# Other order for the weight preparation and the first FFN units in a fused attention and gated FFN kernel

## The chip, the cores and the metric

The kernel runs on one core of one Trainium2 chip. The metric is the device time of one execution in microseconds (us), here the median of three runs. A profiled execution gives the trace from which durations are read. The engines are TensorE (PE in the profile, PEld for its weight loads), VectorE (DVE), ScalarE (ACT), GpSimd (POOL) and SyncE (SP); SP and ACT also issue the transfers.

## The reference, cut to what matters

Eight sequences with eight heads each (64 heads of 576 positions by 64) go through causal attention with a cumulative bias, and all 4608 tokens then through a gated FFN of width 1536:

```python
scores = scale * np.matmul(q, k.transpose(0, 1, 3, 2))
cum = np.cumsum(np.maximum(s, 0.0), axis=-1)
bias = -(cum[:, :, :, None] - cum[:, :, None, :])
scores = np.where(causal, -1000000000.0, scores + np.minimum(bias, 0.0))
attn = np.exp(scores - np.max(scores, axis=-1, keepdims=True))
attn = attn / (np.sum(attn, axis=-1, keepdims=True) + 1e-09)
x = np.matmul(attn, v).transpose(0, 2, 1, 3).reshape(B * S, H * D)
gate = 1.0 / (1.0 + np.exp(-(x @ w_gate)))
return ((gate * (x @ w_val)) @ w_out).astype(np.float32)
```

The three FFN weights arrive as 64-bit floats; the kernel reads them as integers and builds 32-bit floats from their upper halves on the chip.

## The kernel before, in words

**Attention.** One loop over ticks drives everything, five ticks to a head, one for each row tile of the scores, 320 in all. Heads 0 to 7 go through a 32-bit path with transposes on PE. Heads 8 to 63 use operands split into two 16-bit parts: L460 and L461 are the two score matmuls of a piece (six pieces to a head, named s12_3_0 for head 12, tile 3, first column 0), L485 takes the row maximum on DVE, L488 the exponential on ACT, L492 and L497 make the two parts of p, L508 turns p into pt by a transposing DMA on SP, and L520 to L525 multiply pt by v into one PSUM bank, av_bank. L415 swaps halves of the transposed q and k (T). There are two pt buffers of each kind, one buffer of p and one of e. So the maximum of head 12 cannot write e before p of head 11 is made, that not before the transposes of head 10 have read p, and those not before AV of head 8 has freed pt.

**FFN.** The tokens are cut into 18 groups of 256, and a unit is one group and one of twelve slices of 128 of the width. A unit has 24 matmuls 128x256 (L671, into PSUM gv, two buffers), a tanh on ACT (L676), t2 on DVE (L678), the split of the hidden value (L686 ACT, L687 DVE) and, in its "out", six matmuls 128x512 (L701). The first 24 units (groups 0 and 1, named gv0_0 to gv1_11) are written from tick NE = 44 on, FPT slices a tick, in both groups; their t2 wait in one large buffer (t2f) until every weight scale is known (`hidden_scale`), and then the 24 outs follow in a row. All later units follow a fixed share of tokens.

**Weights.** There are 18 weight steps: twelve for w_gate and w_val of a slice, six for two slices of w_out. A step loads 1 MB into a raw buffer (L253 and L260; on SP for the first two steps, on ACT's queue after that), decodes it (L271 on ACT, L273 on DVE), bounds its size (eight Gram matmuls into av_bank, L281 on PE, a row maximum L284 on DVE, a matmul with ones L286 on PE, small DVE steps L129 and L131) and splits it into 16-bit parts (L306 on ACT, L307 on DVE). Before, `weight_step` does all this for step n in one call. The raw buffers are ws0, three pieces of the room that w_out's parts take later (w2all), and two pieces of t2f; the twelve gate steps come first, then the six of w_out. In heads 0 to 7 `min(2 + n // 8, 6)` steps are written by tick n; the others come with the first units, WLA = 3 ahead.

**What orders the work.** The instructions are written in program order by the loop and then placed by a scheduler that runs a model of the time; `first(...)` gives a piece of code a high priority in it, `keep_in_program_order` holds an instruction at its place. `with first(NE <= n < NOFF)` gives it to s_part, av_part and x_part for ticks 44 to 86. Each engine, and SP's and ACT's issue of transfers, is in order.

**x.** The attention output of two heads goes through x16 (a transposing DMA) into one of NX = 10 x slots. NXE = 5 exist from the start, the other five after the first 24 outs (`late_slots`).

Of the kernel before, what the change touches and what calls it, by code (L numbers as in the profile page):

```python
# [25 lines left out]
def tile_attention_then_gated_ffn(  # L26
# [49 lines left out]
    w2all = w2room[:, : 48 * P].bitcast(F16).rearrange("p (f l h x n) -> p f l h x n", f=NF // 2, l=2, h=8, x=2)  # L76
# [113 lines left out]
    ones = lp.tile([P, P], F32, name="ones")  # L190
    nc.gpsimd.memset(ones, 1.0)
    NX, NXE = 10, 5
# [17 lines left out]
    t2big = cp.tile([P, 2 * NF * GT + 4], F32, name="t2f")  # L210
# [10 lines left out]
    raw = [lp.tile([P, RW], I32, name="ws0")] + [w2room[:, i * RW : (i + 1) * RW] for i in range(3)]  # L221
    raw += [t2big[:, 8 * GT + i * RW : 8 * GT + (i + 1) * RW].bitcast(I32) for i in range(2)]
    tops = [lp.tile([P, 8 * P], I32, name="wa0"), rows_out.bitcast(I32)]
# [6 lines left out]
    def room(n):  # L230

        o, f = wsteps[n]
        return outroom[f // 2] if o else (f % 4, n - 3)

    def load_weight(n):
        o, f = wsteps[n]
        fs = slice(f * P, (f + 1) * P)
        r = raw[room(n)[0]]
        for x, src in enumerate((w_out,) if o else (w_gate, w_val)):
            src = src[f * P : (f + 2) * P, :] if o else src[:, fs]  # L240
# [5 lines left out]
            if o == 0:  # L246
                src = src.rearrange("(c p) n -> p c n", p=P)
                dst = dst.rearrange("p (c x n) -> p c x n", c=NC, x=2)[:, :, x]
            else:

                src = src.rearrange("(x p) (h n) -> x p h n", p=P, h=8)
                dst = dst.rearrange("p (h x n) -> x p h n", x=2, h=8)
                ins = nc.scalar.dma_start(dst[0], src[0])  # L253
                if n < NF + 2:
                    tc.keep_in_program_order(ins)
                src, dst = src[1], dst[1]
            if n < 2:
                nc.sync.dma_start(dst, src)
            else:
                ins = nc.scalar.dma_start(dst, src)  # L260
                if n == 2 or NF <= n < NF + 2:
                    tc.keep_in_program_order(ins)

    def decode_weight(n):

        r = raw[room(n)[0]]
        if not wide:
            return r[:, : 8 * P].bitcast(F32), None
        a = tops[n % 2]
        top = a.bitcast(F16).rearrange("p (n t) -> p n t", t=2)[:, :, 1]  # L270
        nc.scalar.activation(top, r.bitcast(BF16)[:, 4:].rearrange("p (n t) -> p n t", t=4)[:, :, 0], AF.Copy)  # L271
        v_ = r[:, : 16 * P].rearrange("p (n t) -> p n t", t=2)[:, :, 1]
        nc.vector.scalar_tensor_tensor(v_, v_, 13, a, ALU.logical_shift_right, ALU.bitwise_or)  # L273
        return v_.bitcast(F32), a

    def square_bound(n, a):

        top = a.bitcast(BF16).rearrange("p (n t) -> p n t", t=2)[:, :, 1]
        ps = av_bank[:, 3 * P :]
        for c in range(8):  # L280
            nc.tensor.matmul(ps, top[:, c * P : (c + 1) * P], top[:, c * P : (c + 1) * P], start=c == 0, stop=c == 7)  # L281
        rows = wp.tile([P, 1], F32, tag="wss", name=f"wrow{n}")
        junk = lp.tile([P, P], BF16, tag="wj", name=f"wj{n}")
        nc.vector.tensor_scalar(junk, ps, 0.0, None, ALU.max, ALU.max, accum_out=rows)  # L284
        tot = av_bank[:, 3 * P - 4 : 3 * P - 3]
        nc.tensor.matmul(tot, ones, rows, start=True, stop=True)  # L286
        return tot

    def split_weight(n, a, m):

        o, f = wsteps[n]
# [5 lines left out]
        if m is None:  # L297
            ss = wp.tile([P, 1], F32, tag="wss", name=f"wss{n}")
            nc.scalar.activation(hi, a, AF.Square, accum_out=ss)
            tot = wp.tile([P, 1], F32, tag="wst", name=f"wtot{n}")  # L300
            nc.gpsimd.partition_all_reduce(tot, ss, P, ADD_REDUCE)
        else:
            tot = square_bound(n, m)
        pow2_of(wscale[:, o, f : f + 1 + o], tot, f"w{n}")
        sc = wscale[:, o, f : f + 1]
        nc.scalar.activation(hi, a, AF.Copy, scale=sc)  # L306
        nc.vector.scalar_tensor_tensor(lo, a, sc, hi, ALU.mult, ALU.subtract)  # L307
# [24 lines left out]
    wnext = {"load": 0, "step": 0}  # L332

    def weight_step():
        n = wnext["step"]
        while n and wnext["load"] < len(wsteps) and room(wnext["load"])[1] < n:
            if not NF <= wnext["load"] < NF + 2:
                load_weight(wnext["load"])
            wnext["load"] += 1
        split_weight(n, *decode_weight(n))  # L340
        wnext["step"] = n + 1

# [319 lines left out]
    def ffn_in(g, f):  # L662
# [14 lines left out]
        t2 = t2first[g * NF + f] if g < 2 else fp.tile([P, GT], F32, tag="t2", name=f"t2_{g}_{f}")  # L677
# [5 lines left out]
    def ffn_mid(g, f):  # L683
        t2 = t2s.pop((g, f))
        h = fp.tile([P, 2, GT], F16, tag="h", name=f"h{g}_{f}", bufs=4)
# [55 lines left out]
    for wnext["load"] in range(2):  # L741
        load_weight(wnext["load"])
    wnext["load"] = 2
# [6 lines left out]
    FPT = 1.5  # L750
    EARLY = 18
    VSQ = 65
    OUT = (22, 30)
    WLA = 3
    nticks = NTL * NH
    for n in range(nticks + 12):
# [43 lines left out]
        if i < NH:  # L800
# [96 lines left out]
            if n in OUT:  # L897
                load_weight(NF + OUT.index(n))
# [67 lines left out]
```

## Time and profile before

| | before |
|---|---|
| runs | 1171.74, 1177.45, 1177.29 us, median 1177.29 |
| profiled execution | 1176.06 us, its span 1174.0 us |
| mean granted TensorE clock | 0.977 |
| PE busy | 1107.9 us (94%) |
| DVE busy | 756.3 us (64%) |
| ACT busy | 736.3 us (63%) |
| POOL busy | 234.3 us (20%) |

Busy is time in which an instruction of the engine was under way; matmuls overlap, so a single one reads longer than the distance of two starts. In a row of windows stand the start and end, the length, the busy time and the number of instructions of each engine, then the granted clock of PE, the busy share of the DMA engines and the GB/s that they moved. In a row of groups stand line, engine, operation, what is written and read, shape and number, then the busy total and the mean in ns of one, then the idle time before such instructions with what ended it. In a row of the timeline stand start and length in us, engine, line, operation and number, and in brackets the idle time before it with its releaser. SPq and ACTq are the issue of transfers by these engines. In a row of waits stand who waits for what, the sum, the number and the longest.

### The profile page before, as it was taken

The numbers are of one execution on the slowest core, as the hardware profiler recorded it, in microseconds if no ns is written. First come the engines' busy times: TensorE is split into PE (matmuls) and PEld (weight loads), VectorE is DVE, ScalarE is ACT, GpSimd is POOL, SyncE is SP. The second block draws the span as 40 slices with busy tenths as digits, with TensorE's granted clock in tenths as the row PEclk, the third lists the DMA queues.
The fourth block names the chain that finished last, engine by engine and source line by source line (L and its number), as shares of the span: only waits on it lengthen the run. The fifth ranks groups of instructions, "written<-read, shape, count | busy, mean of one in ns | idle before, by whom it ended". The sixth has DMA issues, their size and how long they took to land.

```text
span 1174.0 us, 30633 instructions
## 1 busy us (share of the span) xinstructions
PE 1107.9 (94%) x11824; PEld 868.5 (74%) x11824; DVE 756.3 (64%) x2395; ACT 736.3 (63%) x1429; POOL 234.3 (20%) x553
## 2 busy tenths in 40 slices
PE   6897868987999999999999999999999999999998
PEld 4776647754787788778877777778877887787775
DVE  5658765878679687775666677777777775222222
ACT  5877664777678687676666566767776765233222
POOL 4423200223123222221112122222222221000000
PEclk9899879998999999999999999999999999999999
DMA  9777753999899999887565769888978865000000
GB/s 238 207 176 161 157 125 73 205 182 183 174 166 169 162 168 178 158 147 163 93 132 117 128 109 177 161 152 167 159 154 154 153 124 107 12 20 10 10 19 18
DMA packets 445519, 157.64 MB, mean 134 GB/s; under 512 B 403583, under 2 KB 435839, under 8 KB 445374
## 3 DMA queue, kind: packets, MB, share of 16 engines
q1 hardware_dynamic: 418686, 127.38, 61.1%
q10 hardware_dynamic: 23328, 17.04, 5.2%
q0 software_dynamic: 3360, 11.27, 2.9%
q8 instruction: 92, 1.51, 0.5%
q14 instruction: 53, 0.43, 0.1%
HBM read 56.92 MB, written 9.58 MB: 57 GB/s over the span
## 4 chain that ended last, share of the span: by engine, by line
PE 78%; DMA 9%; ACT 5%; DVE 3%; issue 3%; SPq 1%; POOL 1%; ACTq 0%; DVEq 0%; POOLq 0%
PE gv L671 44%; PE o L701 21%; PE s L461 3%; PE s L460 3%; PE av_bank L522 1%; DMA T<-qk 1%; PE av_bank L520 1%; PE av_bank L521 1%; DMA pt<-p 1%; DMA cr<-cum_d 1%; PE s L589 1%; PE na_ps L619 1%; DMA ws<-in_moe_w_out_dram 1%; DMA qk<-in_q_dram 1%; DMA v<-in_v_dram 1%
## 5 line engine op out<-in xcount | busy, mean ns | idle before, releaser
L671 PE MATMUL gv<-x,w 128*128 128x256 f16 (+3 forms) x6912 | 620.2, 248 | 4.4 <-DVE t2f L678 4.4
L671 PEld LDWEIGHTS <-w 128*128 128x128 f16 x6912 | 539.1, 99 | 63.2 <-issue 5.0
L701 PE MATMUL o<-w2all,h 128*128 128x512 f16 x1296 | 315.3, 379 | 0.8 <-ACT io L720 0.8
L475 POOL TENSOR_SCALAR_AFFINE_SELECT rl<-rl 128x64 f32<-128x64 f32 (+1 forms) x280 | 108.7, 389 | 538.7 <-DVE em L485 484.4
L488 ACT ACTIVATE e<-e,em 128x576 f32<-128x576 f32 x280 | 154.3, 554 | 96.3 <-DVE em L485 93.2
L676 ACT ACTIVATE th<-gv,scb 128x256 f32<-128x256 f32 (+3 forms) x288 | 111.0, 411 | 149.5 <-PE gv L671 146.1
L701 PEld LDWEIGHTS <-h 128*128 128x128 f16 x1296 | 123.5, 98 | 107.0 <-issue 0.9
L678 DVE SCALAR_TENSOR_TENSOR t<-th,gv 128x256 f32<-128x256 f32 x192 | 80.2, 418 | 132.0 <-ACT th L676 130.6
L485 DVE CUSTOM_DVE_ANT_0 e<-s,rl,qkcf 128x288 f32<-128x288 f32 x280 | 135.9, 485 | 25.8 <-PE s L461 19.0
L686 ACT ACTIVATE h<-t,hsc 128x256 f16<-128x256 f32 x192 | 96.7, 503 | 79.7 <-DVE t L678 79.6
L497 DVE SCALAR_TENSOR_TENSOR p<-e,p 128x384 f16<-128x384 f32 x224 | 103.3, 501 | 55.9 <-ACT p L492 55.1
L687 DVE SCALAR_TENSOR_TENSOR h<-t,hsc,h 128x256 f16<-128x256 f32 x192 | 93.3, 486 | 45.3 <-ACT h L686 44.8
L492 ACT ACTIVATE p<-e 128x1152 f16<-128x1152 f32 x112 | 112.1, 1000 | 10.4 <-DMA pt<-p 7.9
L460 PE MATMUL s<-T 128*128 128x288 f16 (+2 forms) x246 | 64.8, 280 | 10.8 <-DMA T<-qk 5.0
L520 PE MATMUL av_bank<-v,pt 128*128 128x65 f16 x560 | 69.1, 194 | 5.8 <-DMA pt<-p 5.1
L461 PE MATMUL s<-T 128*128 128x288 f16 (+2 forms) x246 | 62.7, 283 | 9.8 <-DMA T<-T 9.8
L521 PE MATMUL av_bank<-v,pt 128*128 128x64 f16 x560 | 69.0, 193 | 0.0
L522 PE MATMUL av_bank<-v,pt 128*128 128x65 f16 x560 | 68.7, 195 | 0.0
L520 PEld LDWEIGHTS <-pt 128*128 128x128 f16 x560 | 52.7, 98 | 13.7 <-DMA pt<-p 6.3
L423 POOL PARTITION_BROADCAST cr<-cr x63 | 57.9, 921 | 9.6 <-DMA cr<-cum_d 9.6
L521 PEld LDWEIGHTS <-pt 128*128 128x128 f16 x560 | 52.8, 97 | 5.9 <-issue 0.9
L469 DVE TENSOR_SCALAR rl<-cr,qkcf 128x576 f32<-128x576 f32 x56 | 29.2, 522 | 41.1 <-POOL cr L423 40.9
(163 smaller groups left out, 1357.3 us busy)
## 6 DMA issues: line engine op xcount, KB each, us to landing
v<-v SPq DMA_DIRECT2D x56, 162.5 KB
out_dram<-io POOLq DMA_DIRECT2D x34, 256.0 KB, 3.3
v<-in_v_dram SPq DMA_DIRECT2D x64, 128.0 KB
T<-T SPq DMA_DIRECT2D x82, 72.0 KB
t2f<-in_v_dram SPq DMA_DIRECT2D x20, 288.0 KB
qk<-in_q_dram SPq DMA_DIRECT2D x17, 288.0 KB
qk<-in_k_dram SPq DMA_DIRECT2D x17, 288.0 KB
w2all<-in_moe_w_gate_dram ACTq DMA_DIRECT2D x8, 512.0 KB
```

Of the source, the lines that this page charges most:

```text
L460: nc.tensor.matmul(ps[:, : b_ - a], lhs, T[i][:, 0, a:b_], start=True, stop=False)
L461: nc.tensor.matmul(ps[:, : b_ - a], lhs, T[i][:, 2, a:b_], start=False, stop=True)
L475: nc.gpsimd.affine_select(rl[i][:, q0:w], rl[i][:, q0:w], pattern=[[-1, m]], compare_op=ALU.is_ge, fill=-MASKED if i < NN else MASKED, bas ...
L485: nc.vector.tensor_tensor_reduce(e_t[t][:, a:b_], ps[:, : b_ - a], rl[i][:, a:b_], c, init, ALU.add, ALU.min, acc)
L488: nc.scalar.activation(e_t[t][:, :w], e_t[t][:, :w], AF.Exp, bias=init, scale=-1.0)
L492: nc.scalar.activation(p_s[h_][:, 0], e_s[h_], AF.Copy, scale=PSCALE)
L497: nc.vector.scalar_tensor_tensor(flat[:, LOW[t] * P : (LOW[t] + t) * P], e_t[t][:, : t * P], PSCALE, flat[:, kb * P : (kb + t) * P], ALU.m ...
L520: nc.tensor.matmul(AV[i][:, t], hi, v_[:, D : 2 * D + 1], start=kb == 0, stop=False)
L521: nc.tensor.matmul(AV[i][:, t, 0:D], hi, v_[:, 0:D], start=False, stop=False)
L671: nc.tensor.matmul(ps[:, gv, a:e], w1[f][:, cc, gv, wl], x_of(b, cc)[:, xl, c0 + a : c0 + e], start=(c == 0), stop=(c == 3 * NC - 1))
L676: nc.scalar.activation(th[:, a:e], ps[:, 0, a:e], AF.Tanh, scale=scb[b][:, f : f + 1])
L701: nc.tensor.matmul(ps[:m], h[:, hl, tt * P : tt * P + m], w2[f][:, wl], start=(f == 0 and c == 0), stop=(f == NF - 1 and c == 2))
```

## The change

Line numbers after are those of before plus 9 in the attention and FFN code (L460 is L469, L520 is L529, L671 is L680, L701 is L710); the decode is L266 and L268 (L271 and L273 before), the Gram L279, its maximum L283, the ones matmul L288, the split L308 and L309, every weight load L255.

- **Halves.** A call of `weight_step` now loads ahead, decodes step n (with its Gram and row maximum) and then splits step n - 1. The matmul with ones is told to come right behind the newest Gram.
- **Order and buffers.** The 18 steps stand in one list with their raw buffer; w_out's steps are mixed in (8, 10, 4, 6, 0, 2). Six raw buffers: ws0, two pieces of w2all, three of t2f. The decoded tops live in the h ring and the io buffer, ones (now bf16) and a scrap in the t2 ring, which become fixed rings. The two w_out loads at ticks 22 and 30 go.
- **Early steps.** `min(2 + n // 6, 9)` by tick n in place of `min(2 + n // 8, 6)`.
- **First units.** FPT 0.6 in place of 1.5: the 24 units are written over 20 ticks (44 to 63) in place of 8.
- **No priority** for s_part, av_part and x_part in ticks 44 to 86.
- **x.** Seven x slots from the start in place of five; the v square of sequence 2 begins a tick later (VSQ 66).

The core of the diff:

```diff
-    NX, NXE = 10, 5
+    NX, NXE = 10, 7
...
-    wsteps = [(0, f) for f in range(NF)] + [(1, f) for f in range(0, NF, 2)]
-    outroom = [(4, 0), (5, 0), (0, NF - 3), (3, NF - 1), (5, NF + 1), (0, NF + 2)]
+    wsteps = [(0, 0, 0), (0, 1, 1), (0, 2, 2), (0, 3, 3), (0, 4, 0), (0, 5, 1), (1, 8, 4), (0, 6, 2), (0, 7, 3),
+              (1, 10, 5), (0, 8, 4), (0, 9, 1), (0, 10, 0), (0, 11, 2), (1, 4, 5), (1, 6, 1), (1, 0, 0), (1, 2, 5)]
...
     def weight_step():
         n = wnext["step"]
-        while n and wnext["load"] < len(wsteps) and room(wnext["load"])[1] < n:
-            if not NF <= wnext["load"] < NF + 2:
-                load_weight(wnext["load"])
-            wnext["load"] += 1
-        split_weight(n, *decode_weight(n))
+        for m in range(2, min(n + (3 if n < 3 else 4), len(wsteps))):
+            if n and m not in wnext["loaded"] and free_behind[m] <= n - 2:
+                load_weight(m)
+                wnext["loaded"].add(m)
+        words = decode_weight(n) if n < len(wsteps) else None
+        if n:
+            split_weight(n - 1, wnext["words"])
+        wnext["words"] = words
         wnext["step"] = n + 1
...
-    FPT = 1.5
+    FPT = 0.6
...
-            with first(NE <= n < NOFF):
+            with first(False):
                 s_part(i, NTL - 1 - t)
...
-            with first(NE <= n < NOFF):
+            with first(False):
                 av_part(i - 2, 1)
...
-            while n < NE and wnext["step"] < min(2 + n // 8, 6):
+            while n < NE and wnext["step"] < min(2 + n // 6, 9):
                 weight_step()
...
+                if f == 0:
+                    weights_through(gate_step[7])
                 if f < NF and f % WLA == 0:
-                    while wnext["step"] < f + WLA:
-                        weight_step()
+                    weights_through(gate_step[f + WLA - 1])
                     inverse_weights(0, slice(f, f + WLA))
                     ffn_scale(0, slice(f, f + WLA))
-                while f == 8 and wnext["step"] < NF + 1:
-                    weight_step()
-                while f >= NF and wnext["step"] < min(f + NF + WLA, len(wsteps)):
-                    weight_step()
+                if f >= NF:
+                    weights_through(min(gate_step[NF - 1] + 2 * (f - NF + 1), len(wsteps) - 1))
                 emit_unit()
```

**Where instructions stand now.** Three places follow. The first is PE where AV of head 8 begins, before (w1_5 are the split gate and val weights of slice 5, v16_4 the split v of heads 8 and 9):

```order
L671 LDWEIGHTS w1_5_72
L671 MATMUL gv1_5_2191<-x2_135,w1_5_72 128x256
L520 LDWEIGHTS pt1_8_1345
L520 MATMUL av_bank_66<-v16_4_1278,pt1_8_1345 128x65
L521 LDWEIGHTS pt1_8_1345
L521 MATMUL av_bank_66<-v16_4_1278,pt1_8_1345 128x64
```

and after, at the same AV:

```order
L680 LDWEIGHTS w1_3_70
L680 MATMUL gv0_3_1595<-x3_137,w1_3_70 128x256
L529 LDWEIGHTS pt1_8_1393
L529 MATMUL av_bank_66<-v16_4_1304,pt1_8_1393 128x65
L530 LDWEIGHTS pt1_8_1393
L530 MATMUL av_bank_66<-v16_4_1304,pt1_8_1393 128x64
```

AV of head 8 moved up from behind 17 units to behind four. The second place is PE where the scores stop. Before, the last score ahead of the gap is that of head 12, tile 3:

```order
L460 MATMUL s12_3_0_2943<-T12_2805 128x448
L461 LDWEIGHTS T12_2805
L461 MATMUL s12_3_0_2943<-T12_2805 128x448
L671 LDWEIGHTS w1_9_76
L671 MATMUL gv0_9_1844<-x0_133,w1_9_76 128x256
```

and after, where wrow13 is the row bound of weight step 13 and t2 the ones:

```order
L470 MATMUL s13_3_0_3044<-T13_2509 128x448
L680 LDWEIGHTS w1_10_77
L680 MATMUL gv0_10_2045<-x0_134,w1_10_77 128x256
L680 LDWEIGHTS w1_10_77
L680 MATMUL gv0_10_2045<-x0_134,w1_10_77 128x256
L288 LDWEIGHTS t2_131
L288 MATMUL av_bank_66<-wrow13_1966,t2_131 128x1
```

The gap still exists: it begins one head and one unit later. Before, the next score (s12_2_0) comes after 274 unit matmuls, 7 Grams, AV of head 8 and 4 out matmuls. After, the next one (s13_2_0) comes after 336 unit matmuls, 3 Grams, AV of heads 9 to 11 and 81 out matmuls:

```order
L710 MATMUL o1_0_2893<-w2all_79,h_132 128x512
L534 LDWEIGHTS pt0_11_2575
L534 MATMUL av_bank_66<-v32_5_1558,pt0_11_2575 128x64
L469 LDWEIGHTS T13_2509
L469 MATMUL s13_2_0_3112<-T13_2509 128x320
```

From there to the last out of the first 24 (before: 126 unit, 78 score, 140 out and 305 AV matmuls; after: 42, 56, 63 and 200) the stretch has become short of unit work. The third place is ACT at the decodes of w_out words, before (io and wa0 hold the decoded tops; w2all, t2f and ws0 the raw words):

```order
L306 ACTIVATE w2all_79<-t2f_139,wscale_112 128x1024
L260 DMA w2all_79<-in_moe_w_out_dram 128x8x256
L271 ACTIVATE io_138<-w2all_79 128x1024
L253 DMA t2f_139<-in_moe_w_out_dram 128x8x256
L260 DMA t2f_139<-in_moe_w_out_dram 128x8x256
L306 ACTIVATE w2all_79<-ws0_140,wscale_112 128x1024
```

and after, at the last step:

```order
L255 DMA t2f_142<-in_moe_w_out_dram 128x8x256
L685 ACTIVATE th1_1_2260<-gv1_1_2235,scb0_1472 128x256
L308 ACTIVATE w2all_79<-w2all_79,wscale_112 128x1024
L255 DMA t2f_142<-in_moe_w_out_dram 128x8x256
L685 ACTIVATE th1_2_2371<-gv1_2_2346,scb0_1472 128x256
L266 ACTIVATE io_141<-t2f_142 128x1024
L685 ACTIVATE th1_3_2399<-gv1_3_2374,scb0_1472 128x256
```

In both, a decode stands right behind the issue of the load that it reads, or one small instruction later; what has changed is that the tanh of a unit now stands on each side of it.

More of the change, by code (lines that the diff above doesn't have):

```diff
@@ L75, in tile_attention_then_gated_ffn @@
     w2room = cp.tile([P, 48 * P + 6], I32, name="w2all")
-    w2all = w2room[:, : 48 * P].bitcast(F16).rearrange("p (f l h x n) -> p f l h x n", f=NF // 2, l=2, h=8, x=2)
+    w2all = w2room[:, 6:].bitcast(F16).rearrange("p (f l h x n) -> p f l h x n", f=NF // 2, l=2, h=8, x=2)
     w2 = [w2all[:, f // 2, :, :, f % 2] for f in range(NF)]
@@ L189, in tile_attention_then_gated_ffn @@
     lp = lstack.enter_context(tc.tile_pool(name="lp", bufs=1))
-    ones = lp.tile([P, P], F32, name="ones")
+    t2ring = fp.tile([P, 2, GT], F32, name="t2", bufs=1)
+    hring = fp.tile([P, 4, 2, GT], F16, name="h", bufs=1)
+    ones, junk16 = (t2ring[:, i, : P // 2].bitcast(BF16) for i in range(2))
     nc.gpsimd.memset(ones, 1.0)
-    NX, NXE = 10, 5
+    NX, NXE = 10, 7
     xslots = [cp.tile([P, 2, NTL * P], F16, name=f"x{i}") for i in range(NXE)] + [None] * (NX - NXE)
@@ L209, in tile_attention_then_gated_ffn @@
     rows_out = cp.tile([P, 2 * DM], F32, name="io")
-    t2big = cp.tile([P, 2 * NF * GT + 4], F32, name="t2f")
+    t2big = cp.tile([P, 2 * NF * GT + 6], F32, name="t2f")
     t2first = [t2big[:, u * GT : (u + 1) * GT] for u in range(2 * NF)]
@@ L273, in decode_weight, with square_rows @@
         nc.vector.scalar_tensor_tensor(v_, v_, 13, a, ALU.logical_shift_right, ALU.bitwise_or)
-        return v_.bitcast(F32), a
-    def square_bound(n, a):
+        square_rows(n, a)
+        return v_.bitcast(F32)
+    wrow, wlast = {}, {}
+    def square_rows(n, a):
         top = a.bitcast(BF16).rearrange("p (n t) -> p n t", t=2)[:, :, 1]
@@ L280, in square_bound, with split_weight @@
         for c in range(8):
[L281 to L284, printed above, removed]
+            ins = nc.tensor.matmul(ps, top[:, c * P : (c + 1) * P], top[:, c * P : (c + 1) * P],
+                                   start=c == 0, stop=c == 7)
+        wlast["gram"] = ins.ins
+        wrow[n] = wp.tile([P, 1], BF16, tag="wss", name=f"wrow{n}")
+        nc.vector.tensor_scalar(junk16, ps, 0.0, None, ALU.max, ALU.max, accum_out=wrow[n])
+    def square_bound(n):
         tot = av_bank[:, 3 * P - 4 : 3 * P - 3]
-        nc.tensor.matmul(tot, ones, rows, start=True, stop=True)
-        return tot
-    def split_weight(n, a, m):
-        o, f = wsteps[n]
+        with tc.issue_after(wlast["gram"]):
+            nc.tensor.matmul(tot, ones, wrow.pop(n), start=True, stop=True)
+        return tot
+    def split_weight(n, a):
+        o, f, _ = wsteps[n]
         if o:
@@ L296, in split_weight @@
             hi, lo = (w1[f].rearrange("p c g l n -> p (c g) l n")[:, :, l] for l in range(2))
-        if m is None:
-            ss = wp.tile([P, 1], F32, tag="wss", name=f"wss{n}")
+        if n not in wrow:
+            ss = wp.tile([P, 1], F32, tag="wsq", name=f"wss{n}")
             nc.scalar.activation(hi, a, AF.Square, accum_out=ss)
@@ L330, in out_scale, with weights_through @@
         nc.vector.tensor_scalar(osc[b], gmax, sv[b][1], 2.0 ** 14, ALU.mult, ALU.mult)
-    wnext = {"load": 0, "step": 0}
+    wnext = {"step": 0, "loaded": set(), "words": None}
     def weight_step():
         n = wnext["step"]
-        while n and wnext["load"] < len(wsteps) and room(wnext["load"])[1] < n:
-            if not NF <= wnext["load"] < NF + 2:
-                load_weight(wnext["load"])
-            wnext["load"] += 1
-        split_weight(n, *decode_weight(n))
+        for m in range(2, min(n + (3 if n < 3 else 4), len(wsteps))):
[6 more added lines that the diff above has]
+        wnext["words"] = words
         wnext["step"] = n + 1
+    def weights_through(n):
+        while wnext["step"] <= n + 1:
+            weight_step()
     def ffn_scale(b, fs=slice(0, NF)):
@@ L676, in ffn_in @@
             nc.scalar.activation(th[:, a:e], ps[:, 0, a:e], AF.Tanh, scale=scb[b][:, f : f + 1])
-        t2 = t2first[g * NF + f] if g < 2 else fp.tile([P, GT], F32, tag="t2", name=f"t2_{g}_{f}")
+        t2 = t2first[g * NF + f] if g < 2 else t2ring[:, f % 2]
         nc.vector.scalar_tensor_tensor(t2[:, :n], th[:, :n], 1.0, ps[:, 1, :n], ALU.add, ALU.mult)
@@ L684, in ffn_mid @@
         t2 = t2s.pop((g, f))
-        h = fp.tile([P, 2, GT], F16, tag="h", name=f"h{g}_{f}", bufs=4)
+        h = hring[:, f % 4]
         nc.scalar.activation(h[:, 0], t2, AF.Copy, scale=hsc[:, f : f + 1])
@@ L740, in tile_attention_then_gated_ffn @@
     n_load(0)
-    for wnext["load"] in range(2):
-        load_weight(wnext["load"])
-    wnext["load"] = 2
+    for n in range(2):
+        load_weight(n)
     load_crow(0)
```

44 lines of the change are left out of this document (18 added, 26 removed).

## The prediction

> **What bounds the kernel now.** I read the page first (engine totals, the span in 40 slices), then the windows of the stages between the jumps seen there, then in the weak stages the maximum of the scores, the waits and the timelines.
>
> ```profile
> span 1174.0 us, 30633 instructions
> PE 1107.9 (94%) x11824; PEld 868.5 (74%) x11824; DVE 756.3 (64%) x2395; ACT 736.3 (63%) x1429; POOL 234.3 (20%) x553
> PE   6897868987999999999999999999999999999998
> PEclk9899879998999999999999999999999999999999
> ```
>
> PE is the bound from the tenth slice (some 290 us) on. Earlier there are holes, and the clock dips with them. The windows give their size (from and to, length, busy time of PE, PEld, DVE, ACT, POOL, clock, DMA share, GB/s):
>
> ```profile
> 0.00:105.00 105.00, 87.26 (x605) 72.38 (x606) 63.27 (x205) 76.60 (x152) 39.70 (x103) 0.93 0.81 194
> 105.00:157.00 52.00, 39.04 (x320) 30.93 (x319) 41.83 (x135) 38.32 (x62) 13.72 (x24) 0.90 0.79 170
> 157.00:205.00 48.00, 36.09 (x321) 29.67 (x320) 27.59 (x76) 22.41 (x31) 0.41 (x1) 0.82 0.39 88
> 205.00:291.00 86.00, 71.14 (x739) 47.19 (x738) 69.80 (x227) 60.34 (x112) 24.38 (x56) 0.96 1.03 190
> 345.00:1000.00 655.00, 653.16 (x7522) 515.36 (x7521) 475.27 (x1547) 452.83 (x886) 142.65 (x341) 1.00 0.80 147
> ```
>
> From 345 us to 1000, 653.16 of 655 us are busy: nothing there can be won, and the change leaves the order alone there. The time is the work of PE plus its idle and slow time before 291 us. The score maxima (L485 on DVE, 12 records to a head) show what goes wrong:
>
> ```profile
> 0.00:105.00 105.00, 1.79 (x6) 0.93 0.81 194
> 105.00:157.00 52.00, 10.33 (x42) 0.90 0.79 170
> 157.00:205.00 48.00, 0.00 (x0) 0.82 0.39 88
> 205.00:291.00 86.00, 20.52 (x80) 0.96 1.03 190
> ```
>
> From 157 to 205 us attention stands still, with DVE at 27.59 of 48 us and DMA at 0.39. Then it crowds at a DMA share of 1.03. The transfers stand at a pt transpose that waits for PE (the SP queue's issues and the row of its waits):
>
> ```profile
> 156.38 0.60 SPq L415 DMA_DIRECT2D T<-T  x1
> 202.91 4.35 SPq L508 DMA_TRANSPOSE pt<-p  x2
> SPq L508 <- PE gv L671: 42.8, 2, 42.2
> ```
>
> pt is free when AV of head 8 has read it, and that AV is written behind 17 units. Meanwhile PE waits for the weight steps: Grams and ones matmuls on PE, the load and decode of w_out on ACT, and the stretch as a window.
>
> ```profile
> 157.12 0.62 PE L281 MATMUL av_bank<-io 128*128 128x128 bf16 x8
> 161.63 0.56 PE L286 MATMUL av_bank<-wrow,ones 128*128 128x1 f32 x2 [1.91 <-DVE wj L284]
> 164.97 1.01 PE L281 MATMUL av_bank<-io 128*128 128x128 bf16 x8 [2.79 <-DVE xe_w L129]
> 169.25 0.55 ACTq L260 DMA_DIRECT2D w2all<-in_moe_w_out_dram  x1
> 173.96 1.35 ACT L271 ACTIVATE io<-w2all 128x1024 f16<-128x1024 bf16 x1 [4.40 <-DMA w2all<-in_moe_w_out_dram]
> 157.00:171.00 14.00, 6.54 (x50) 5.06 (x49) 10.75 (x34) 9.09 (x12) 0.41 (x1) 0.67 0.48 106
> ```
>
> PE is busy 6.54 of 14 us, at a clock of 0.67.
>
> **The change part by part.** I split the time from 105 us (head 8's first maxima) to 291.24 us, where the last early out is done and unit work fills PE again, into three stages, and sum the changed program's stages against these 186.2 us.
>
> *Before head 8.* The order shows one decode and one split more by then (9 and 6 against 8 and 5).
>
> ```profile
> L271 ACT ACTIVATE io<-w2all 128x1024 f16<-128x1024 bf16 x7 | 9.5, 1358 | 5.5 <-DMA w2all<-in_moe_w_out_dram 4.4 <-DMA w2all<-in_moe_w_val_dram 1.1
> L306 ACT ACTIVATE w<-w2all,wscale 128x1024 f16<-128x1024 f32 x9 | 11.0, 1227 | 1.1 <-DVE wscale L131 1.1
> L273 DVE SCALAR_TENSOR_TENSOR w2all<-w2all,io 128x1024 int32<-128x1024 int32 x7 | 8.6, 1225 | 6.8 <-ACT io L271 6.8
> L307 DVE SCALAR_TENSOR_TENSOR w<-w2all,wscale,w 128x1024 f16<-128x1024 f32 x9 | 11.6, 1286 | 3.5 <-ACT w L306 3.4
> 0.00:25.00 25.00, 16.43 (x94) 12.64 (x94) 12.04 (x32) 12.56 (x24) 12.25 (x39) 1.00 1.03 242
> ```
>
> That is 1.36 + 1.23 = 2.6 us of ACT and 1.23 + 1.29 = 2.5 us of DVE, beside 28 and 42 idle us of these engines in 0 to 105; if none of it hides, +2.6. On the other side the 1 MB load of step 2 no longer opens ACT's queue: at 242 GB/s, in a stretch where DMA is full (1.03), 1 MB is 4.1 us that the first q and k can land earlier. Bounds -4 to +3, taken: **-1**, as engine time hides better than a full queue.
>
> *Stage A, head 8's maxima to the new stop (head 13, tile 3).* It holds 54 records of L485 (five heads less the six before 105 us) and ten units, 240 matmuls. Before, 42 records took 52 us, 1.24 us a record, beside these units (L671 alone):
>
> ```profile
> 105.00:157.00 52.00, 30.45 (x221) 23.03 (x220) 0.90 0.79 170
> ```
>
> At that pace 54 make 66.9. DVE, busy 41.83 of 52 us, would need 41.83 x 54/42 = 53.8 if it never waited. Units per record fall by 16%, but three steps more (7.5 us of DVE) lie in it. I take **63**, nearer to the pace (54 to 70).
>
> *Stage B, the gap.* AV of heads 9 to 11 and 81 outs now fill the gap beside 14 units: 336 unit matmuls, 120 AV, 81 out and 24 Gram matmuls stand between s13_3 and s13_2. Distances of starts, from a full stretch and from the AV run after the gap:
>
> ```profile
> 602.98 2.78 PE L671 MATMUL gv<-x,w 128*128 128x256 f16 x24
> 605.60 1.46 PE L701 MATMUL o<-w2all,h 128*128 128x512 f16 x6
> 606.89 0.25 PE L460 MATMUL s<-t2f 128*128 128x192 f16 x1
> ...
> 207.20 0.19 PE L520 MATMUL av_bank<-v,pt 128*128 128x65 f16 x1
> ...
> 208.23 0.19 PE L521 MATMUL av_bank<-v,pt 128*128 128x64 f16 x1
> ```
>
> A unit takes 605.60 - 602.98 = 2.62 us (109 ns a matmul), an out 1.29 (215 ns), 36 AV starts 1.03 (29 ns), a Gram 0.62/8 = 78 ns. So 336 x 0.109 + 81 x 0.215 + 120 x 0.029 + 24 x 0.078 = 36.6 + 17.4 + 3.5 + 1.9 = 59.4 us. Seven splits remain, a half step behind their Grams, and attention's DVE and ACT work has stopped, so I add 2.6 for decode and bound waits (one of the 2.79 us waits above): **62** (59 to 77).
>
> *Stage C, the rest of heads 13 to 18.* 28 score pieces, 4.67 heads, with only 42 unit and 63 out matmuls. Before, 80 records, 6.67 heads, took 86 us: 12.9 a head, 60 for 4.67. PE work is no bound here: 42 x 0.109 + 63 x 0.215 + 200 x 0.029 + 56 x 0.11 = 30 us. DVE's 69.80 us for 6.67 heads, 10.5 a head, gives 49 if DVE never waited. Heads wait for transfers:
>
> ```profile
> 284.81 1.04 PE L461 MATMUL s<-T 128*128 128x288 f16 x3 [2.57 <-DMA T<-T]
> 289.45 0.24 PE L520 MATMUL av_bank<-v,pt 128*128 128x65 f16 x1 [2.80 <-DMA pt<-p]
> 291.24 5.04 PE L671 MATMUL gv<-x,w 128*128 128x192 f16 x54
> ```
>
> Fewer outs share DVE and ACT than before, but the transfers of a head stay as many. I take the middle, **54.5**.
>
> *Rest.* At the end of C the changed program has done the same units, outs and Grams as the old one at 291.24 us, but 10 score matmuls and 25 AV matmuls fewer, by the counts of the order. A score matmul has 267 columns on average, about 0.11 us by the 109 ns for 256; so 10 x 0.11 + 25 x 0.029 = 1.8 us, which PE makes up later at full load. Break-even for A + B + C is thus 186.2 - 1.8 = 184.4. The x slots, the later v square and the fixed rings cost nothing here: they add no instruction, and the trace shows no wait of theirs in these stages; without that cover one slot wait would cost a v load, 2 to 3 us. Dropping the priority works only through the order, which is counted.
>
> Sum: 63 + 62 + 54.5 = 179.5, that is -4.9, and -1 from before head 8: -5.9 on the profiled 1176.06 gives **1170 us**. The profile lies 1.2 us below the median of the runs, 1177.29; from that it is -0.6%. A measurement of this kernel can tell about 0.5%, 5.9 us, from no change.
>
> [...] In 157 to 171 us, with PE busy less than half, the clock was 0.67, and in the first stall it was lower still:
>
> ```profile
> 25.00:40.00 15.00, 11.80 (x53) 9.72 (x53) 9.25 (x28) 11.63 (x22) 5.72 (x13) 0.54 0.98 258
> ```
>
> Stage C has 30 us of PE work in 54, about the same share. If the clock falls to 0.67 through it, the work takes 30/0.67 = 45 us, 15 more. [...] But 45 still fits into 54.5, since transfers, not PE, hold the pace: only what sits between two transfers (scores, AV) lengthens. Taken in the sum: 0; if all of it is on the path: 1185.
>
> **The rivals.**
> - *Forecast's case*, 1166 to 1174: as above.
> - *The gap is filled without a hole and attention runs at DVE's pace*: A 60, B 59.4, C 51 give 170.4, 14.0 under break-even, and 1 more: 1161. For it: attention and units are spread, and DVE was at 0.57 in the gap. Against: the DMA share of 1.03.
> - *The gain is given back in C*: heads stay at 12.9 us each, C 60, and the sum is 185, 0.6 over break-even, less 1: 1176. For it: DMA at 1.03 did not let 6.67 heads through faster, and the change only moves the stop, not removes it.
> - *The weight loads come late (slower)*: four decodes (steps 13, 15, 16 and 17) stand on ACT right behind the issue of what they read. The row above has decode 4.7 us after issue (173.96 - 169.25); with about 1 us of work between, 3.7 us a wait, four make 15. Behind them wait the tanh that free gv, hence PE. If all are on PE's path: 1170 + 15 = 1185. It decides from 13 us on, nearly all four, where 1177.29 + 5.9 is passed. Against: gv has two buffers, and outs need no tanh.
> - *The clock falls in C (slower)*: 1185, as worked out; it decides from about 13 of the 15 us on the path, where 1177.29 + 5.9 is passed. Against: at 205 to 291 us the clock was 0.96, with waits of the same kind in it.
>
> **How the numbers follow.** Forecast's case 0.36, three quarters of it below 1171.4 (0.5% under the median); gap filled 0.18; given back 0.21; late loads 0.15; clock 0.10. Faster 0.27 + 0.18 = 0.45; same 0.09 + 0.21 = 0.30; slower 0.25. The range 1159 to 1186 leaves out what lies beyond the filled gap (a third of its 0.18) and the worse part of the two slow cases (0.12).
>
> **What would show it.** Right: the maxima stop at head 13 and not 12, some 10 us later than 157; the stop holds PE above 90% for about 62 us; then 4.67 heads in 50 to 58 us; from there rows match before's at about 5 us less. Wrong in B: PE idle behind ACT waits for w_out. Wrong in C: clock under 0.8, or over 12.5 us a head. Wrong altogether: a new wait in 0 to 105 us, or a hole after 300 us, where I have put nothing.

## The result and the profile after

The changed kernel is slower: 1193.17 us (median of four runs, 1190.35 to 1194.7) against 1175.4 us for the kernel before in the same comparison, a ratio of 1.0135 (95% interval 1.0103 to 1.0167). The forecast was 1170 us, in a range of 1159 to 1186. The profiled execution took 1194.09 us. Experiments 6 and 12 below had one much longer, slow execution each (1300.38 and 2929.86 us), which their ratios leave out and their medians count.

The page of the kernel after, its span, totals, slices and clock:

```profile
span 1192.3 us, 30651 instructions
PE 1116.7 (94%) x11806; PEld 865.4 (73%) x11806; DVE 757.0 (63%) x2395; ACT 736.2 (62%) x1429; POOL 235.7 (20%) x553
PE   6798687894899999999999999999999999999998
PEclk8999799997999999999999999999999999999999
```

The busy time of DVE, ACT and POOL is that of before. PE is busy 9 us longer, and idle 9 us longer, the latter in the first twelve slices. The tenth slice, some 270 to 300 us, is now the thinnest of all (4 tenths).

To hold the trace against the forecast, the windows have to be cut where the forecast cut. Its 105 us lies between the third and the fourth of head 8's six maxima; that place is now at 111 us. Its gap B is what PE does between the score matmuls s13_3 and s13_2, now the 74.2 us from 174.84 to 249.07. Its stage C ends where unit work fills PE again, now at 301 us (300.80, before 291.24). The windows of the kernel after, with the bare part of C as a row of its own:

```profile
0.00:111.00 111.00, 87.64 (x587) 71.26 (x588) 65.16 (x211) 78.39 (x155) 41.89 (x102) 0.92 0.80 197
111.00:175.00 64.00, 47.73 (x419) 37.85 (x418) 53.90 (x175) 47.98 (x78) 16.38 (x32) 0.85 0.81 155
175.00:249.00 74.00, 63.36 (x566) 46.66 (x564) 37.92 (x106) 35.65 (x62) 4.61 (x11) 0.97 0.51 112
249.00:301.00 52.00, 35.77 (x365) 22.55 (x364) 39.44 (x129) 32.08 (x56) 15.71 (x34) 0.82 0.94 177
265.00:301.00 36.00, 19.77 (x259) 14.60 (x256) 26.40 (x91) 22.15 (x37) 11.67 (x27) 0.74 0.96 177
360.00:1000.00 640.00, 639.34 (x7322) 499.49 (x7320) 465.18 (x1515) 442.72 (x870) 140.06 (x336) 1.00 0.79 148
```

In three of them the score maxima (L494 now), and in the last two of these the outs (L710):

```profile
111.00:175.00 64.00, 13.28 (x54) 0.85 0.81 155
175.00:249.00 74.00, 1.78 (x6) 0.97 0.51 112
249.00:301.00 52.00, 13.01 (x52) 0.82 0.94 177
175.00:249.00 74.00, 18.49 (x81) 7.49 (x81) 0.97 0.51 112
249.00:301.00 52.00, 15.24 (x64) 5.57 (x63) 0.82 0.94 177
```

Stage A holds the 54 records of the forecast, the 74 us of the gap B six, and C 52, four heads and a third. The gap has the 81 outs that the order showed. One thing in the order was read wrongly: the counts of the section on the change "to the last out of the first 24" run on to the place where unit work resumes. The last early out starts at some 278 us in the kernel before and at 265 us after, so the last 36 us of C have no out at all, and PE is busy there 19.77 us. From 360 us on PE is full, as before. Stage by stage:

| stage | forecast | measured |
|---|---|---|
| start to head 8's third maximum | 104 (105 less 1) | 111 |
| A, to the stop | 63 | 64 |
| B, the gap | 62 | 74 |
| C, to the return of unit work | 54.5 | 52 |
| the rest, against 882.8 before | +1.8 | +8.5 |

B is 12 us over. The start and the rest, 7 us each, are taken up in the part on the prediction. In B, PE is idle for 10.6 us. The rows of its waits (175 to 249 us) say that units wait for the t2 of an earlier unit, and Gram matmuls (L279) for decodes and for the bound of the step before:

```profile
PE gv L680 <- DVE t2f L687: 4.5, 5, 2.4
PE av_bank L279 <- ACT io L266: 4.0, 2, 2.3
PE av_bank L279 <- DVE xe_w L129: 1.9, 1, 1.9
```

On ACT the decodes (L266) in turn wait for w_out loads. Two pieces of the timeline of the kernel after, PE first:

```profile
179.95 0.64 PE L279 MATMUL av_bank<-io 128*128 128x128 bf16 x8 [1.68 <-ACT io L266]
...
188.81 0.62 PE L279 MATMUL av_bank<-h 128*128 128x128 bf16 x8 [1.85 <-DVE xe_w L129]
...
202.08 0.63 PE L279 MATMUL av_bank<-io 128*128 128x128 bf16 x8 [2.33 <-ACT io L266]
...
212.11 3.12 PE L680 MATMUL gv<-x,w 128*128 128x256 f16 x27 [2.44 <-DVE t2f L687]
```

The bound of the preceding step is what the Gram at 188.81 waits for. ACT, and DVE just ahead of 212.11:

```profile
180.85 0.55 ACTq L255 DMA_DIRECT2D ws<-in_moe_w_out_dram  x1
...
186.09 1.35 ACT L266 ACTIVATE h<-ws 128x1024 f16<-128x1024 bf16 x1 [2.86 <-DMA ws<-in_moe_w_out_dram]
189.20 1.22 ACT L308 ACTIVATE w2all<-t2f,wscale 128x1024 f16<-128x1024 f32 x1 [1.45 <-DVE wscale L131]
191.78 0.55 ACTq L255 DMA_DIRECT2D t2f<-in_moe_w_out_dram  x1
196.11 0.55 ACTq L255 DMA_DIRECT2D t2f<-in_moe_w_out_dram  x1
200.68 1.34 ACT L266 ACTIVATE io<-t2f 128x1024 f16<-128x1024 bf16 x1 [3.45 <-DMA t2f<-in_moe_w_out_dram]
...
210.32 1.28 DVE L309 SCALAR_TENSOR_TENSOR w2all<-t2f,wscale,w2all 128x1024 f16<-128x1024 f32 x1
...
211.68 0.71 DVE L687 SCALAR_TENSOR_TENSOR t2f<-th,gv 128x256 f32<-128x256 f32 x2
```

This is a chain: the decode of step 16 (186.09) waits for its load and stands ahead of the split of step 14 (189.20); that split frees the raw buffer of load 17, whose second half is issued at 196.11 and read at 200.68. The outs cannot begin before the last split, since their scale needs every weight scale. Nor can the last eight of the 24 units be finished: the program puts their t2 into the very part of t2f that holds load 17 (the third raw piece of t2f is the room of units 16 to 23). The first two of these t2 are made at 211.68, right behind the last split on DVE (210.32); by then both gv buffers are full, and PE stands for 2.44 us.

That accounts for the place of the largest loss in this trace. It does not yet say which edit made the whole slower, since the gap before also had such waits. Two theories went into the experiments. **P**: the missing priority. The early outs are placed in the gap, where attention stands, and are missing afterwards, when attention runs alone and leaves PE half empty. **W**: the weights, by late w_out loads and by more steps before head 8. The slower rest behind 301 us belongs to neither.

### The profile page after: what moved, and what is told of

It reads as the page before. It is cut to its first block, busy times and chain, and to the rows that moved or that the text cites. A ratio compares the mean times of both kernels' runs of the same rounds, so it can differ in the third digit from the quotient of the medians.

```text
span 1192.3 us, 30651 instructions
## 1 busy us (share of the span) xinstructions
PE 1116.7 (94%) x11806; PEld 865.4 (73%) x11806; DVE 757.0 (63%) x2395; ACT 736.2 (62%) x1429; POOL 235.7 (20%) x553
## 4 chain that ended last, share of the span: by engine, by line
PE 71%; DMA 11%; issue 7%; DVE 4%; ACT 4%; POOL 2%; SPq 1%; ACTq 0%; POOLq 0%; DVEq 0%
PE gv L680 39%; PE o L710 21%; PE s L469 2%; PE s L470 2%; DMA T<-qk 2%; DMA pt<-p 2%; PE av_bank L531 1%; PE av_bank L529 1%; PE av_bank L530 1%; DMA cr<-cum_d 1%; DMA ws<-in_moe_w_out_dram 1%; DMA w2all<-in_moe_w_gate_dram 1%; DMA T<-T 1%; DVE e L494 1%; DMA t2f<-in_moe_w_out_dram 1%
## 5 line engine op out<-in xcount | busy, mean ns | idle before, releaser
L680 PE MATMUL gv<-x,w 128*128 128x256 f16 (+3 forms) x6912 | 613.6, 247 | 6.7 <-DVE t2f L687 5.2
L680 PEld LDWEIGHTS <-w 128*128 128x128 f16 x6912 | 537.3, 98 | 66.8 <-issue 6.7
L710 PE MATMUL o<-w2all,h 128*128 128x512 f16 x1296 | 320.9, 382 | 0.0
L710 PEld LDWEIGHTS <-h 128*128 128x128 f16 x1296 | 120.9, 96 | 112.2
L494 DVE CUSTOM_DVE_ANT_0 e<-s,rl,qkcf 128x288 f32<-128x288 f32 x280 | 135.6, 486 | 26.9 <-PE s L470 20.1
L469 PE MATMUL s<-T 128*128 128x288 f16 (+2 forms) x246 | 66.6, 287 | 13.4 <-DVE em L494 10.8
L529 PE MATMUL av_bank<-v,pt 128*128 128x65 f16 x560 | 69.9, 195 | 7.5 <-DVE xq L544 5.3
L470 PE MATMUL s<-T 128*128 128x288 f16 (+2 forms) x246 | 64.2, 287 | 8.7 <-DMA T<-T 8.7
L529 PEld LDWEIGHTS <-pt 128*128 128x128 f16 x560 | 53.4, 99 | 16.8 <-issue 7.2
L730 POOL DMA_DIRECT2D out_dram<-io x34 | 19.4, 571 | 189.8 <-ACT io L729 189.0
```

The lines of the kernel that those rows point to most:

```text
L494: nc.vector.tensor_tensor_reduce(e_t[t][:, a:b_], ps[:, : b_ - a], rl[i][:, a:b_], c, init, ALU.add, ALU.min, acc)
L529: nc.tensor.matmul(AV[i][:, t], hi, v_[:, D : 2 * D + 1], start=kb == 0, stop=False)
L680: nc.tensor.matmul(ps[:, gv, a:e], w1[f][:, cc, gv, wl], x_of(b, cc)[:, xl, c0 + a : c0 + e], start=(c == 0), stop=(c == 3 * NC - 1))
L710: nc.tensor.matmul(ps[:m], h[:, hl, tt * P : tt * P + m], w2[f][:, wl], start=(f == 0 and c == 0), stop=(f == NF - 1 and c == 2))
```

## The experiments

Ratios are against the kernel before, run beside each; in brackets 95% intervals.

**1. The priority put back** into the changed kernel:

```diff
-            with first(False):
+            with first(NE <= n < NOFF):
```

> The changed kernel with the priority for scores, AV and x of ticks 44 to 86 put back. Theory P (the missing priority lets the 24 outs be placed in the gap of attention, so that heads 15 to 18 then run alone with PE half empty): the outs are spread over heads 13 to 18 again, the 25 us that PE loses between the last early out and 305 us fall to about 11, and the time is 1176 to 1182 us. Theory W (late w_out loads and more weight steps before head 8 cost the time): within 4 us of the changed kernel, 1189 to 1196.

Measured: 1178.75 us, 1.0023 [0.9999, 1.0047]. Theory P holds: with one switch the loss of 1.35% is down to what cannot be told from nothing. The windows of this run, the gap and the mixed stage behind it:

```profile
169.00:217.00 48.00, 38.03 (x358) 31.30 (x358) 28.79 (x82) 26.91 (x46) 2.30 (x6) 0.86 0.56 130
217.00:286.00 69.00, 61.86 (x589) 39.24 (x587) 54.31 (x178) 46.05 (x87) 19.28 (x42) 0.98 0.96 173
```

and in the second window the outs (L710) and the maxima (L494):

```profile
217.00:286.00 69.00, 35.53 (x144) 13.33 (x142) 0.98 0.96 173
217.00:286.00 69.00, 15.13 (x60) 0.98 0.96 173
```

All 144 out matmuls run beside sixty maxima, five heads, in 69 us, with PE at 61.86. The gap is 48 us, not 74: it holds one out, not 81, and 240 unit matmuls, not 336.

**2. The priority taken from the kernel before**, and nothing else:

```diff
-            with first(NE <= n < NOFF):
+            with first(False):
```

> The kernel before with only the priority of ticks 44 to 86 taken away. Theory P (without it the outs go into the gap and heads 13 to 17 run alone afterwards, whatever the weight steps and the pace of the units are): PE loses some 25 us between the last early out and head 19 where it lost 12, and the time is 1187 to 1194 us. Rival (the priority matters only together with the other edits): 1173 to 1181.

Measured: 1203.34 us, 1.0240 [1.0204, 1.0277], more than P had said. Its outs (L701) and maxima (L485) in two windows each, and the whole of the second:

```profile
217.00:264.00 47.00, 34.54 (x144) 13.56 (x142) 0.93 0.59 108
264.00:322.00 58.00, 1.46 (x6) 0.57 (x6) 0.74 0.93 169
```

```profile
217.00:264.00 47.00, 3.31 (x13) 0.93 0.59 108
264.00:322.00 58.00, 14.67 (x60) 0.74 0.93 169
```

```profile
264.00:322.00 58.00, 35.52 (x458) 27.74 (x457) 44.52 (x151) 37.62 (x66) 17.66 (x40) 0.74 0.93 169
```

This is the mechanism in its pure form. The outs take 47 us with 13 maxima beside them, then five heads take 58 us with hardly an out beside them: 105 us for 73 maxima and the outs. Mixed, in experiment 1, sixty maxima and the outs took 69 us; at that pace per maximum 73 would take 84, an estimate, 21 us less than 105. (The two stretches differ in other work too, above all in AV.) PE is busy 35.52 of the 58 us, at a clock of 0.74.

**3. Units over 20 ticks and no priority**, on the kernel before:

```diff
-    FPT = 1.5
+    FPT = 0.6
...
-            with first(NE <= n < NOFF):
+            with first(False):
```

> The kernel before with units over 20 ticks and no priority, and nothing else of the change. Theory P: these two numbers make the whole loss, since the weight steps are as before: 1186 to 1196 us. Theory W (the new weight order is half of the loss): 1180 to 1185.

Measured: 1193.82 us, 1.0157 [1.0131, 1.0184]: as much as the changed kernel loses, with the old weight steps, old buffers and five x slots. That the two figures agree is in part chance, since the changed kernel has costs and gains of its own (experiments 6 to 10 and the pace of the outs below).

**4. Units over 20 ticks alone**, on the kernel before, with the priority:

> The kernel before with one number changed: the first 24 units over 20 ticks. Theory P: with the priority kept, AV of head 8 moves up, head 13's first scores are reached before the gap and the outs stay mixed with attention; the part of the change that was forecast to gain does gain: 1164 to 1172 us. Rival (the slower units only move the gap): within 4 us of before, 1172 to 1180.

Measured: 1177.01 us, 1.0008 [0.9984, 1.0031]. The rival holds: the slower pace that was forecast to be the gain gains nothing here. It helps only where the priority is missing (1.0157 against 1.0240).

These runs and the result make a table of ratios:

| | priority | none |
|---|---|---|
| weights of before, 8 ticks | 1 | 1.0240 |
| weights of before, 20 ticks | 1.0008 | 1.0157 |
| changed weights, slots and ticks | 1.0023 | 1.0135 |

Down the left column nothing can be told from 1; each step to the right costs 1.1 to 2.4%.

**5. No priority, but the outs one to a tick.** The priority touches scores, AV and x, not outs. Whether it works through the outs was open:

```diff
                 hidden_scale()
-                while state["o"] < 2 * NF:
-                    emit_out()
                 late_slots()
+        elif n >= NE and state["o"] < 2 * NF:
+            emit_out()
```

> The changed kernel, still without the priority, whose 24 early outs are written one to a tick (ticks 64 to 87) and not all at once behind the last early unit. Theory P by its mechanism (the outs are spent while attention stands, and are missed when it runs): the outs now stand among heads 13 to 18, and the time is 1176 to 1183 us, as with the priority back. Rival (the priority matters by where it puts scores and AV, not by the outs): 1188 to 1195.

Measured: 1183.36 us, 1.0045 [1.0017, 1.0073], just above what P had said. The late x slots now come ahead of the outs; that is the only other thing the edit moves. Two thirds of the loss (1.35% to 0.45%) go when the outs are spread by the program alone. For the maxima (L494) and the engines from the first outs on:

```profile
222.00:297.00 75.00, 15.33 (x61) 0.93 0.80 160
222.00:297.00 75.00, 68.94 (x720) 47.88 (x719) 55.98 (x177) 47.50 (x89) 20.08 (x41) 0.93 0.80 160
```

Five heads run beside 129 of the 144 outs again, and PE is busy 68.94 of 75 us. The rest, up to the run with the priority, may be the scores' own place; no run tells that.

**6. The late loads left out** of the changed kernel (three loads are not made, so the output is not the reference's):

```diff
-                load_weight(m)
+                if m < 15:
+                    load_weight(m)
```

> The changed kernel without the loads of the last three weight steps (15, 16 and 17), which decode what an earlier step left in the buffer: 3 MB of loads are left out. Theory W: the waits of ACT for w_out at these decodes (1.4, 2.9 and 3.5 us, and 1.5 us of a tanh behind the issue) go, and PE's idle time behind them: 6 to 10 us less, 1183 to 1187 us. Theory P: the units and outs only get into the gap sooner, heads 13 to 18 still run alone: 0 to 4 us less, 1189 to 1193.

Measured: 1185.83 us, 1.0076 [1.0033, 1.0118], some 7 us less than the changed kernel (the intervals of the two ratios overlap a little). The time is in W's band and not in P's, so the late loads have a part in the loss.

**7. The same with the priority back:**

> The changed kernel with the priority back and without the loads of the last three weight steps (3 MB of loads are left out). If the two causes add, 1178.75 less 7 to 8: 1169 to 1173 us. If the priority hides the waits behind attention's matmuls: 1175 to 1180.

Measured: 1159.1 us, 0.9872 [0.9838, 0.9906]. Neither band had this: 19.7 us less than with the priority alone, more than twice what the loads gave without it. A reading that fits, and that no run isolates: without the priority a shorter gap brings on the bare stage sooner, but not shorter; with it, the outs that start sooner go among the heads. The gap and the stage behind it in this run:

```profile
171.00:202.00 31.00, 29.62 (x314) 24.92 (x314) 24.46 (x74) 23.05 (x41) 1.16 (x4) 0.95 0.54 106
202.00:269.00 67.00, 61.78 (x601) 41.28 (x599) 51.73 (x166) 45.20 (x82) 19.38 (x40) 1.00 1.03 181
```

The gap is full (29.62 of 31 us) and ends with head 13's first maximum; in the first run it takes 44 us to that (169 to 213).

**8. The late loads sent elsewhere.** Leaving loads out removes waits and bytes. Here the last three go to a DRAM room that nobody reads, with the same issues and bytes. They wait for no buffer there, so the last two issues go out at 181 us, where they went out at 191 and 196 with the priority alone:

```diff
+            if n >= 15:
+                dst = w_spare[n - 15, :, :, x]
```

> The changed kernel with the priority back, whose last three weight loads go to a DRAM room that nobody reads, at about their old places; the decodes read what an earlier step left. All 3 MB are moved and issued, only the waits for them are gone. If the waits cost (theory W): 1157 to 1165 us, near the run without the loads. If the bytes cost, by taking room on the DMA engines: 1172 to 1180.

Measured: 1165.6 us, 0.9895 [0.9864, 0.9926], just above the band of W. So most of the 19.7 us are the waits: 13 us by the medians, 15 by the ratios (1.0023 less 0.9895). Whether the bytes cost anything is not shown, since the intervals of this run and of the one without the loads overlap.

**9. The loads left out of the kernel before:**

> The kernel before without the loads of its last three weight steps (3 MB of loads are left out). If the w_out waits cost before as much as they cost the changed kernel with the priority back (19.7 us without those loads), the old order had the same weak place and the new order did not mend it: 1154 to 1162 us. If the old order hid them: 1168 to 1176.

Measured: 1173.17 us, 0.9951 [0.9914, 0.9989], 4 us (6 by the ratio). The old order had hidden most of it: the late w_out loads weigh more in the new order, as 19.7 us against 4 say.

**10. The split ahead of the decode** from step 15 on, with the priority back, to break the chain shown above:

```diff
+        if n >= 15:
+            split_weight(n - 1, wnext["words"])
         words = decode_weight(n) if n < len(wsteps) else None
-        if n:
+        if 0 < n < 15:
             split_weight(n - 1, wnext["words"])
```

> The changed kernel with the priority back and, from step 15 on, the split of step n - 1 written ahead of the decode of step n. In the changed kernel the decode of step 16, which waits for its load, stands ahead of the split of step 14, which frees the buffer of load 17. Theory W (the chain load 16, decode 16, split 14, load 17, decode 17 is what costs): the last load starts some 8 us sooner, and the time is 1164 to 1173 us. Rival (the wait only moves to the decode of step 16): 1175 to 1180.

Measured: 1172.59 us, 0.9942 [0.9916, 0.9967]. This is the first version with all its loads that beats both kernels, by 0.6%, at the upper edge of W's band. In the ACT timeline of this run the last load's second half is issued 11 us behind that of step 16, where it was 15 (180.85 and 196.11 in the kernel after) and 17 with the priority alone. The decodes of both still wait:

```profile
181.62 0.55 ACTq L255 DMA_DIRECT2D ws<-in_moe_w_out_dram  x1
182.54 1.24 ACT L308 ACTIVATE w2all<-t2f,wscale 128x1024 f16<-128x1024 f32 x1 [0.99 <-DVE wscale L131]
186.48 1.35 ACT L266 ACTIVATE h<-ws 128x1024 f16<-128x1024 bf16 x1 [2.70 <-DMA ws<-in_moe_w_out_dram]
187.50 0.55 ACTq L255 DMA_DIRECT2D t2f<-in_moe_w_out_dram  x1
192.64 0.55 ACTq L255 DMA_DIRECT2D t2f<-in_moe_w_out_dram  x1
...
199.59 1.34 ACT L266 ACTIVATE io<-t2f 128x1024 f16<-128x1024 bf16 x1 [2.92 <-DMA t2f<-in_moe_w_out_dram]
```

**11. The last steps further apart.** Two tries at the same waits by the program's spacing, the first with two units between steps from unit 10 on, the second with the split first, load 17 issued right behind it, and one step to a unit:

> The changed kernel with the priority back and the last four weight steps written two units apart, from unit 10 on, in place of two steps to a unit from unit 12 on. Theory W: a w_out load then lands while a unit's work stands between its issue and its decode, and of the 7 us that leaving the loads out gave, some 4 to 8 come: 1170 to 1175 us. Theory P alone: no change against the run with the priority back, 1176 to 1182.

> As the run before, and the last steps one to a unit, not two. Theory W: units stand between a load and its decode, so the waits of ACT shrink further: 1162 to 1172 us. Rival (it is not the waits but the later last split, which holds all outs back): slower than the run before by 3 to 8 us.

Measured: 1185.85 us, 1.0084 [1.0057, 1.0111], and 1174.64 us, 0.9970 [0.9949, 0.9990]. The first is a miss on both theories: against the run with the priority alone the time is 7 us longer, not shorter. The decode of load 17 waits longer here, 5.8 us (2.8 with the priority alone): its two halves are issued at 196.00 and 200.35 us, behind the splits of steps 14 and 15 (192.32 and 198.95), and the outs wait for its own split. In the waits of ACT in this run (165 to 222 us):

```profile
ACT io L266 <- DMA t2f<-in_moe_w_out_dram: 5.8, 1, 5.8
ACT h L266 <- DMA ws<-in_moe_w_out_dram: 5.1, 1, 5.1
```

The profile of this run was 6 us late at head 8 already, where the program is the same; how much of the 7 us belongs to the spacing stays open. The second cannot be told from experiment 10 and is in neither of its bands; its last decode waits 1.3 us, not 2.9, and nothing is gained by it.

**12. The early steps at their old pace** in the changed kernel:

```diff
-            while n < NE and wnext["step"] < min(2 + n // 6, 9):
+            while n < NE and wnext["step"] < min(2 + n // 8, 6):
```

> The changed kernel with the weight steps of heads 0 to 7 paced as before (2 + n // 8, up to 6). Theory E (the faster pace costs the 8 us that PE has lost more than before by head 8's first maximum): that loss falls to about 2 and the time to 1184 to 1188 us. Rival: the three steps come back as waits at tick 44, since unit 0 needs step 8: head 8 starts earlier but the first unit later, and the time stays within 3 us, 1190 to 1196.

Measured: 1215.42 us, 1.0315 [1.0268, 1.0363]: a miss on both sides. Head 8 does start sooner (97 us), but the steps come back in the first heads of the 16-bit path. In this run and in the kernel after, from head 8's first maximum on:

```profile
97.00:148.00 51.00, 27.05 (x201) 19.57 (x199) 39.10 (x122) 34.53 (x54) 11.04 (x24) 0.73 0.92 189
```

```profile
106.00:150.00 44.00, 32.07 (x273) 25.27 (x272) 36.51 (x112) 34.03 (x54) 12.22 (x21) 0.78 0.92 173
```

PE is busy 53% of the time where it was 73%. The faster early steps are thus needed by the new order; taking them back is no cure for the loss.

**13. Split first and outs one to a tick**, with the priority:

> The changed kernel with the priority back, the split ahead of the decode from step 15 on, and the outs one to a tick. If spreading the outs by the program gives more than the priority gives: 1164 to 1170 us. If the priority has done it already: 1170 to 1176, as without the spreading.

Measured: 1173.65 us, 0.9960 [0.9936, 0.9984]: the priority has done it already.

## Why the prediction was wrong

The differences of the stage table add up to the 24 us between the forecast and the profile: 7 before head 8, 1 in A, 12 in B, 2.5 less in C and 7 in the rest.

**Before head 8 (-1): not shown wrong.** The profiles of kernels with the same start differ by as much as the 7 us. Head 8's first maximum stands at 101 us in the profile before and at 106 in that after. In all five profiles with the old start it lies between 101 and 107 us, 104.4 in the mean; in the ten with the changed start between 102 and 109, 104.9 in the mean. So one profile cannot tell this term, and most of the 7 us is the luck of two profiles.

**A (63) and C (54.5): right,** at 64 and 52 us. The heads in C took 12.0 us each, between the two bounds, as it was reasoned. In windows of 2 us the clock there is 1.00 until 275 us and, behind an idle stretch of PE of 4.8 us that ends there, 0.50 to 0.53 in eight of the thirteen up to 301. What lowers it is not shown by any run. The forecast's step that a slower clock would not lengthen C holds: it took 52 us at a mean clock of 0.82. Its reason, that transfers hold the pace, is not shown: of the waits of PE from 265 to 301 us, 14.0 us are put down to DVE and 2.1 to transfers.

**B (62, up to 77): the step that failed.** The dense work was put at 59.4 us, and the trace has the counted matmuls. What stands beside it was put at 2.6 us, and the trace has 74.2 - 59.4 = 14.8, of which 10.6 are idle time of PE. This is the rival of the late loads (15 us, a chance of 0.15), with its place and nearly its price. The argument against it was that gv has two buffers and that outs need no tanh. It failed because PE did not wait for the tanh alone: it stood at Grams that need the decode itself (4.0 us); the last eight units could not leave gv before the last split (a wait of 2.44 us), as their t2 lies in the room of load 17; and the outs stood behind that split as well (the first at 218.57 us). For the last steps, the half step between decode and split made it worse, as experiment 10 shows by turning it round. Experiment 6 prices the late loads at 7 of the 12 us; the other 5 stay open.

**The rest, and "the fixed rings cost nothing": a term put at nothing that measures some 6 us.** Behind 301 us the profile takes 8.5 us longer than before behind 291.24, and the forecast had 1.8 for the matmuls made up there (the trace has 8 score and 23 AV matmuls more, near the 10 and 25 of the forecast). The outs are slower. The last 24 of the program, before and after:

```profile
1164.14 5.34 PE L701 MATMUL o<-w2all,h 128*128 128x512 f16 x24
1182.38 5.46 PE L710 MATMUL o<-w2all,h 128*128 128x512 f16 x24
```

These are 5 ns a matmul, 6 us for all 1296 by an estimate; the busy time of the 1296 is 315.3 and 320.9 us. The unit right ahead of them takes 2.62 us in both kernels (1161.52 to 1164.14, and 1179.76 to 1182.38), so PE as a whole is not slower there. It is no chance of one profile: all five profiles with the old weight code have 5.34, all eleven with the changed one 5.46. What does it is open. The outs read w2all and h, and the change moved both: h became a fixed ring, and w2all begins 24 bytes later in its room (`w2room[:, 6:]`), an edit that the section on the change does not list. No run separates them.

**"Dropping the priority works only through the order, which is counted": what was not asked.** It was counted, and the bare stage C came out as reasoned. What was not asked is what the same outs would give in another place. Experiments 1 to 4 show that its absence costs 1.1 to 2.4% in all three rows of the table, and experiment 5 that most of it goes through the outs: in the changed kernel 81 of 144 are spent in the gap and the others in the first 16 us of C, and then attention leaves PE at 20 of 36 us. With the priority, the rest of the change sums to nothing that can be told (1.0023), with the late loads and the slower outs among its costs.

**"The gain is the fuller gap": wrong as a gain.** The forecast took outs in the gap for PE time that is no longer idle. That is so, and the gap is not shorter for it: the same work is then missing in C. Mixed in, the outs cost, roughly and across two kernels, some 11 us on top of five heads (69 us in experiment 1 against 58 in experiment 2); on their own they took most of the 47 us of experiment 2.

## What to carry to other kernels

Work that waits for nothing is a filler, and its worth depends on where it is spent: here the heads behind the gap, with PE busy 19.77 of 36 us, needed the outs more than the gap did (experiments 1 and 5). Before crediting a change with a hole that it fills, follow the filler to the place from which it was taken. And where a load waits for a buffer, look for the instruction that frees it, and for what stands ahead of that instruction on its own queue: moving only the reader in the program gained nothing in the two tries here. Last, where PE is the bound, compare the pace of the same matmuls before and after: 5 ns each was 6 us here, and no wait shows it.

## What the runs showed of the hardware

Five heads with hardly an out ran in 58 us at a granted clock of 0.74, 11.6 us a head, and five heads with all outs in 69 us at 0.98. In the kernel before, heads with outs and units beside them took 12.9 us each at 0.96. A slow clock thus stood beside heads that were no slower, with PE idle for 22 of those 58 us. In the kernel after, PE was idle for 16 of the 36 us without outs (265 to 301 us, clock 0.74), and its waits there are put down to DVE (14.0 us) and to transfers (2.1 us).

The same out matmul, 128x512, took 5 ns longer in every kernel with the changed buffers (24 in 5.46 us, not 5.34). With the priority (1178.75 us), leaving 3 MB of late loads out gave 20 us (1159.1), and moving the same bytes where nobody waits for them 13 (1165.6); what the bytes alone cost lies within the noise.
